# Linear attention in 64-token blocks instead of 128, inside a fused attention and MLP kernel

## The chip, the cores and the metric

The kernel runs on one core of a Trainium2 chip. The metric is the device time of one execution in microseconds; lower is better. The kernel before took 193.41 us (median of three runs, 192.16 to 193.62).

The names of the engines in the profile: PE is the matrix engine (PEld its weight loads), DVE the vector engine, ACT the scalar (activation) engine, POOL the GpSimd engine, SP the engine that issues most transfers. PSUM is the memory that PE writes into, in banks; SBUF is the working memory.

## What is computed

Four batches, eight heads, 768 tokens, head size 64. A decaying linear attention, written in blocks of 64 tokens, feeds an MLP of width 512 to 2048 to 512 with a quick GELU:

```python
block = 64
rel = pos[:, None] - pos[None, :]
Dmask = np.where(rel >= 0, lam[:, None, None] ** rel[None, :, :], 0.0)
lam_pow = lam[:, None, None] ** (pos[None, :, None] + 1)
for b in range(nb):
    intra = np.einsum('bhic,bhjc->bhij', qb, kb) * Dmask[None]
    intra = np.einsum('bhij,bhjd->bhid', intra, vb)
    inter = np.einsum('bhid,bhde->bhie', qb * lam_pow[None], kv_state)
    out[:, :, sl] = intra + inter
    rev_pow = lam[:, None, None] ** (block - 1 - pos[None, :, None])
    kv_state = lam_block * kv_state + np.einsum('bhsd,bhse->bhde', kb * rev_pow, vb)
x = attention output, (3072, 512)
h = x @ w_in                              # 512 to 2048
out = (h * sigmoid(1.702 * h)) @ w_out    # 2048 to 512
```

The block length is a free choice: a longer block moves work from the state into the masked scores, with the same result.

## The kernel before

The 3072 tokens are worked in six waves of 512. Waves 0 and 1 take 256 tokens of two batches each and have functions of their own (names with d_). Waves 2 to 5 take 128 tokens of all four batches; their functions begin with n_ and are what the change touches. Matrices are in bf16, sums in f32 in PSUM.

**Attention of a wave (2 to 5).** Heads are laid out in pairs on the 128 partitions, rows A = 0 to 63 and Z = 64 to 127. One block is the whole 128 tokens.
- `n_scores` (L335): for each of four head pairs p, eight matmuls that contract over 64 rows and give scores of 128 x 128 tokens for one batch and one head.
- `n_masks` (L345): scores times a power of lambda for each row (inv_pow) and a triangle of ones and zeros. There are two ways: "M" does it in one DVE instruction (L354), "m" scales on ACT (L350) and multiplies on DVE (L351).
- `n_rest` (L377): state times q (inter, L383), masked scores times v on top of it in the same PSUM bank (intra, `n_out`, L396), ACT copies the result to xT (L400), and then `n_state` (L363) sums keys times values over all 128 tokens (L370) and DVE adds this to the decayed old state (L374). The state is held twice (kv_sb) and written for the next wave.

**MLP of a wave.** Both products are done as seven products of halves with sums before and after (a Strassen form). The first: four groups a, b, c, d, each with products 1 to 7 (`in_product`, L548; matmuls at L561) and a GELU (A to D, `in_gelu`, L580). The second: `product` (L454, matmuls at L470) with n = 1 to 7 and t = 0, 1 for two token halves. Its sums of g are made on DVE ("gl1" to "gl4" for the low, "gh1" to "gh4" for the high half, L447). Its banks are Q (product 2), V (7, then 4 on top) and X (1, 6, 5, 3, one on top of the other). So product 5 may only add into X when product 6's value has been copied out of it, and product 3 when product 5's has been read. `after_product` (L480) does the copies on ACT (products 1, 6, 7, L486) and the sums on DVE (2, 4, 5, L502); a sum of product 4 waits there for the copy of product 6, and product 2's sum is put off to the step "o". Outputs leave through SP (L510).

**What sets the order.** The order on every engine is written out by hand: `STEPS[w]` (L633) lists for wave w the products of its MLP between the attention steps of wave w + 1. Each engine runs its instructions in that order and waits where data or a buffer are not ready. The letters: "a1", "b7" and so on are products of the first matmul, "P40" is product 4 for t = 0, "S" and "M" or "m" are scores and masks, "v0", "v1" the casts of v to bf16 for batches 0, 1 and 2, 3 (both on ACT, L224), "R" is `n_rest`, "K", "Q", "t" prepare the next k and q, "L" issues loads, "X" makes sums of xT for the next MLP ("+a1" is that next wave's product).

PSUM is handed out in two rings: tag "a" with five banks (scores, attention outputs, states, some products) and "mm" with three.

Of the kernel before, what the change touches and what calls it, by code (L numbers as in the profile page):

```python
# [25 lines left out]
def kernel(  # L26
# [13 lines left out]
    nc = tc.nc  # L40
# [3 lines left out]
    P = 128  # L44
# [67 lines left out]
    def iota(x, pattern, base, cm):  # L112
        nc.gpsimd.iota(x, pattern=pattern, base=base, channel_multiplier=cm, allow_small_or_imprecise_dtypes=True)
# [20 lines left out]
    iota(i_q, [[0, 1]], 1, 1)  # L134
    mask = work.tile([P, 1, P], bf16, tag="mask", bufs=1, name="mask")
    nc.gpsimd.memset(mask, 1.0)
# [30 lines left out]
    inv_pow = const.tile([P, H], f32)  # L167
    blk_pow = const.tile([P, NP], f32)
    warm = const.tile([P, 1], f32)
# [124 lines left out]
    def d_keep(w, c):  # L294
        nc.scalar.copy(kv_sb[1][:, 2 * w + c], states[w, c])
        if w:
            kept[w, c] = work.tile([P, NP, D], f32, tag="half", bufs=1, name="half")
            nc.scalar.copy(kept[w, c], states[w, c])
# [36 lines left out]
    def n_scores(w, p):  # L335
        s2 = [acc("ps_s") for _ in range(2)]
        for b in range(B):
            kT, qT = trans[w, b // 2, "k"], trans[w, b // 2, "q"]
            for h in range(2):
                hs = slice(64 * h, 64 * h + 64)  # L340
                nc.tensor.matmul(s2[h][:, b, :], kT[hs, (b % 2) * NP + p, :], qT[hs, (b % 2) * NP + p, :],  # L341
                                 start=True, stop=True)
        masked[w, p] = s2

    def n_masks(w, p, split=False):  # L345
        for h, s in enumerate(masked.pop((w, p))):
            sm = work.tile([P, B, P], bf16, tag="sm", bufs=8, name="sm")
            n = 4 * (p // 2) + 2 * h + p % 2
            if split:
                nc.scalar.activation(sm, s, COPY, scale=inv_pow[:, n : n + 1])  # L350
                nc.vector.tensor_tensor(sm, sm, mask.to_broadcast([P, B, P]), op=MUL)  # L351
                masked[w, p, h] = sm
                continue
            nc.vector.scalar_tensor_tensor(sm, s, inv_pow[:, n : n + 1],  # L354
                                           mask.to_broadcast([P, B, P]), op0=MUL, op1=MUL)
            masked[w, p, h] = sm

    def n_two(w, pp):
        for f in (n_scores, n_masks):
            for p in (2 * pp, 2 * pp + 1):  # L360
                f(w, p)

    def n_state(w, R):  # L363
        ps_kv = acc("ps_kv", shape=[P, 2, B, D])
        new, old = kv_sb[(w + 1) % 2], kv_sb[w % 2]
        for i in range(2):
            for b in range(B):
                for j, js in enumerate((A, Z)):
                    n0 = (2 * R + i) * P + j * D
                    nc.tensor.matmul(ps_kv[js, i, b, :], cast[w, b // 2, "k"][:, b % 2, n0 : n0 + D],  # L370
                                     v_sb[w % 2][:, b, 4 * R + 2 * j + i, :], start=True, stop=True)
        for i in range(2):
            p = 2 * R + i
            nc.vector.scalar_tensor_tensor(new[:, :, p, :], old[:, :, p, :], blk_pow[:, p : p + 1], ps_kv[:, i],  # L374
                                           op0=MUL, op1=ADD)

    def n_rest(w):  # L377
        kv, o = kv_sb[w % 2], [acc("ps_o") for _ in range(NP)]
        for R in range(2):
            for b in range(B):  # L380
                for i, cs in enumerate((A, Z)):
                    for j, js in enumerate((A, Z)):
                        nc.tensor.matmul(o[2 * R + j][cs, b, :], kv[js, b, 2 * R + i, :],  # L383
                                         trans[w, b // 2, "q"][js, (b % 2) * NP + 2 * R + i, :],
                                         start=(b == 0), stop=False, skip_group_check=True)
        for p in range(NP):
            n_out(w, p, o[p])
        if w + 1 < NW:
            for R in range(2):
                n_state(w, R)  # L390

    def n_out(w, p, ps_o):
        vt, R, j = v_sb[w % 2], p // 2, p % 2
        for b in range(B):
            for i, cs in enumerate((A, Z)):
                nc.tensor.matmul(ps_o[cs, b, :], vt[:, b, 2 * p + i, :], masked[w, 2 * R + i, j][:, b, :],  # L396
                                 start=False, stop=True, skip_group_check=True)
        if w not in xT:
            xT[w] = xp.tile([P, NP, W], bf16, tag="x", name="xT")
        nc.scalar.copy(xT[w][:, p, :], ps_o.rearrange("p b s -> p (b s)"))  # L400
# [181 lines left out]
    def one_step(w, s):  # L582
# [30 lines left out]
        elif s[0] == "m":  # L613
            n_masks(x, int(a), True)
        elif s[0] == "R":
            n_rest(x)
# [13 lines left out]
        else:  # L630
# [27 lines left out]
    with tc.manual_schedule():  # L658
        for x, i in ((k_pow, i_k), (q_pow, i_q)):
            nc.scalar.activation(x, ln_lam.unsqueeze(1).to_broadcast([P, 2, H]), EXP, scale=i)  # L660
        mk_pow(inv_pow, -1.0 * P)
# [39 lines left out]
        for pp in range(2):  # L701
            d_scores(0, 1, pp)
            d_masks(0, 1, pp)
        nc.gpsimd.affine_select(mask, mask, pattern=[[0, 1], [1, P]], channel_multiplier=-1, base=0,
                                compare_op=mybir.AluOpType.is_ge, fill=0.0)
# [116 lines left out]
```

## Time and profile before

| what | value |
| --- | --- |
| median of three runs | 193.41 us |
| profiled execution | 193.18 us |
| its span | 191.4 us |
| one wave, from one first score stretch to the next (94.07 to 122.10) | 28.03 us |
| busy in that wave: PE, DVE, ACT, POOL | 28.03, 24.62, 20.81, 8.23 us |

How to read the lines below. The page's first part gives each engine's busy time, its share of the span and the number of instructions; the second shows busy tenths in 40 equal slices. The chain of waits goes back from the last instruction to whatever released it: start, length, engine, tile and line, count. A row of the timeline has start, length, engine, line, operation, output and inputs, count, and in brackets the engine's idle time before it and who ended it. A row of a group has its count, then busy time in all and the mean length of one in ns, then idle time before. PE matmuls overlap, so the mean length of one is longer than the step from one to the next.

### The profile page before, as it was taken

Reading aid. Unit: us, or ns where it says so; the run is one execution under the profiler, and the core shown is the slowest. Engines: PE = TensorE matmul, PEld = TensorE weight load, DVE = VectorE, ACT = ScalarE, POOL = GpSimd, SP = SyncE. Lnnn points to the kernel's source line nnn. Section 1 sums busy time; section 2 is a strip of 40 time slices with the busy share of each in tenths; the row PEclk is TensorE's granted clock in tenths of the full one; section 3 lists DMA queues with packets and bytes.
Section 4 is the critical chain, followed back from the end, with each engine's and each line's share of the span. In section 5 each row is a group of like instructions: output and inputs, shape, how many; then the busy total and the mean of one; then the engine's idle time right before and its main releaser. Section 6 shows DMA issues by size and latency. Waiting matters only on the chain.

```text
span 191.4 us, 5525 instructions
## 1 busy us (share of the span) xinstructions
PE 184.1 (96%) x2295; PEld 151.9 (79%) x2295; DVE 152.0 (79%) x282; ACT 129.9 (68%) x242; POOL 51.2 (27%) x69
## 2 busy tenths in 40 slices
PE   7888999999999999999999999999999999999993
PEld 2556646877888888888888888888888888888882
DVE  3687289997965799879799879799789797888950
ACT  6766764168776986389896288885488876597611
POOL 5588000046449000195000294000493000000000
PEclk9999999999999999999999999999999999999999
DMA  5999999996998899768999455999365803300113
GB/s 144 320 281 194 203 206 204 284 312 178 232 265 184 193 225 255 191 161 154 218 233 229 165 146 132 224 254 254 107 156 126 202 4 113 110 5 0 54 58 110
DMA packets 89599, 33.91 MB, mean 177 GB/s; under 512 B 67430, under 2 KB 89446, under 8 KB 89574
## 3 DMA queue, kind: packets, MB, share of 16 engines
q1 hardware_dynamic: 84676, 28.84, 60.4%
q0 software_dynamic: 4896, 4.72, 14.5%
q8 instruction: 18, 0.29, 0.6%
q14 instruction: 7, 0.06, 0.1%
q10 hardware_dynamic: 2, 0.00, 0.0%
HBM read 27.26 MB, written 6.29 MB: 175 GB/s over the span
## 4 chain that ended last, share of the span: by engine, by line
PE 76%; DMA 9%; DVE 8%; POOL 3%; ACT 1%; SPq 1%; issue 0%; ACTq 0%
PE ps_X L470 20%; PE ps_hX L561 16%; PE ps_V L470 9%; PE ps_hV L561 8%; DMA w_in<-in_moe_w_in_dram 7%; PE ps_Q L470 5%; PE ps_hQ L561 4%; PE ps_h L420 4%; DVE w_out_t L434 3%; DVE g_s L447 3%; DMA qf<-in_q_dram 2%; PE ps_s L341 2%; PE ps_o L396 2%; POOL w_in L184 2%; PE ps_o L383 1%; DVE w_in_t L537 1%
## 5 line engine op out<-in xcount | busy, mean ns | idle before, releaser
L470 PEld LDWEIGHTS <-g_s 128*128 128x128 bf16 x384 | 37.0, 98 | 4.8
L580 ACT ACTIVATE g_sb<-h_sb 128x512 bf16<-128x512 f32 x54 | 32.6, 631 | 1.2 <-DVE h_sb L569 1.2
L470 PEld LDWEIGHTS <-g_sb 128*128 128x128 bf16 x288 | 27.5, 98 | 4.4 <-issue 0.3
L561 PEld LDWEIGHTS <-w_in_t 128*128 128x128 bf16 x288 | 28.1, 98 | 3.3
L224 ACT COPY part<-ps_hX 128x512 f32<-128x512 f32 x32 | 18.3, 586 | 11.5 <-PE ps_hX L561 11.5
L470 PE MATMUL ps_X<-w_out_t,g_s 128*128 128x256 bf16 x192 | 23.3, 273 | 0.0
L561 PEld LDWEIGHTS <-w_in 128*128 128x128 bf16 x216 | 21.1, 98 | 2.5
L561 PE MATMUL ps_hX<-x_s,w_in_t 128*128 128x256 bf16 x144 | 21.6, 272 | 0.0
L447 DVE TENSOR_TENSOR g_s<-g_sb 128x1024 bf16<-128x1024 bf16 x24 | 16.2, 686 | 5.8 <-ACT g_sb L580 5.6
L212 POOL TENSOR_TENSOR ks<-kf,k_pow 128x512 bf16<-128x512 f32 x16 | 16.3, 1042 | 4.5 <-DMA kf<-in_k_dram 4.5
L212 POOL TENSOR_TENSOR qs<-qf,q_pow 128x512 bf16<-128x512 f32 x16 | 16.7, 1069 | 2.7 <-DMA qf<-in_q_dram 2.7
L221 DVE COPY part<-ps_hV 128x512 f32<-128x512 f32 x18 | 12.4, 688 | 5.9 <-PE ps_hV L561 5.9
L653 POOL CAST behind_q<-x_s 1x1 f32<-1x1 bf16 x3 | 0.5, 176 | 58.5 <-DVE x_s L546 58.5
L486 ACT COPY part<-ps_X 128x512 f32<-128x512 f32 (+1 forms) x13 | 6.7, 518 | 13.5 <-PE ps_X L470 13.5
L569 DVE TENSOR_TENSOR h_sb<-part,ps_hX 128x512 f32<-128x512 f32 x18 | 12.2, 680 | 2.6 <-PE ps_hX L561 2.1
L569 DVE TENSOR_TENSOR h_sb<-part,ps_hV 128x512 f32<-128x512 f32 x18 | 12.3, 683 | 1.0 <-PE ps_hV L561 1.0
L470 PE MATMUL ps_X<-w_out,g_sb 128*128 128x256 bf16 x96 | 12.6, 272 | 0.2 <-DMA w_out<-in_moe_w_out_dram 0.2
L470 PE MATMUL ps_Q<-w_out,g_sb 128*128 128x256 bf16 x96 | 12.5, 273 | 0.0
L569 DVE TENSOR_TENSOR h_sb<-part,ps_hQ 128x512 f32<-128x512 f32 x18 | 12.2, 678 | 0.0
L224 ACT CAST v_sb<-vf 128x1024 bf16<-128x1024 f32 (+1 forms) x14 | 11.9, 866 | 0.2 <-DMA vf<-in_v_dram 0.2
L580 ACT ACTIVATE g_sb<-ps_hX 128x512 bf16<-128x512 f32 x18 | 10.6, 588 | 1.8 <-PE ps_hX L561 1.8
L420 PE MATMUL ps_h<-xT,w_in 128*128 128x256 bf16 x96 | 11.3, 273 | 0.3 <-DMA w_in<-in_moe_w_in_dram 0.3
(113 smaller groups left out, 354.1 us busy)
## 6 DMA issues: line engine op xcount, KB each, us to landing
kf<-in_k_dram SPq DMA_DIRECT2D x10, 512.0 KB, 6.6
qf<-in_q_dram SPq DMA_DIRECT2D x10, 512.0 KB, 6.7
vf<-in_v_dram SPq DMA_DIRECT2D x10, 512.0 KB, 6.1
out_dram<-o_sb SPq DMA_DIRECT2D x24, 128.0 KB, 2.5
out_dram<-o_sb SPq DMA_DIRECT2D x12, 256.0 KB, 2.5
w_out<-in_moe_w_out_dram POOLq DMA_DIRECT2D x4, 512.0 KB, 15.4
kf<-in_k_dram SPq DMA_DIRECT2D x4, 256.0 KB, 3.1
qf<-in_q_dram SPq DMA_DIRECT2D x4, 256.0 KB, 4.5
```

Of the source, the lines that this page charges most:

```text
L184: nc.gpsimd.dma_start(out=w_in_sb[j], in_=moe_w_in.rearrange("(kc ki) f -> ki kc f", ki=P)[:, :, c0 : c0 + IN_CH[j] * P])
L212: eng.tensor_tensor(x.rearrange("p b (r i j d) -> p j (b r) i d", i=2, j=2, d=D)[:, j], f.rearrange("p h (a d) -> p (h a) d", a=2).rearran ...
L221: nc.vector.tensor_copy(out, in_)
L224: nc.scalar.copy(out, in_)
L420: nc.tensor.matmul(h[:, u, :], w_in_sb[j][:, kc, i * P : (i + 1) * P], xT[w][:, kc, cols], start=(kc == 0), stop=(kc == KC - 1))
L434: nc.vector.tensor_tensor(o, x, y, op=SUB)
L447: nc.vector.tensor_tensor(o, x, y, op=f)
L470: nc.tensor.matmul(bank[:, t], x[:, m, t * P : (t + 1) * P], y, start=((n in (1, 2, 7) or own) and t == ts[0] * last and m == 0), stop=(m ...
L486: nc.scalar.copy(part[w, n, t.start][:, t], bank[:, t])
L561: nc.tensor.matmul(bank[:, u], z[:, kc], y[:, kc], start=(n in (1, 2, 7) and u + kc == 0), stop=(kc == 1), skip_group_check=True)
L569: nc.vector.tensor_tensor(h, h_part[w, g, {2: 1, 5: 7, 4: 6}[n]], bank, op=ADD)
L580: nc.scalar.activation(g_of[w][:, a : b + 1 : b - a, 256 * i : 256 * i + 256], bank, GELU)
```

## The change

Attention of waves 2 to 5 goes to blocks of 64 tokens. Scores are 64 x 64 for each of the two blocks (a wave has both blocks of all pairs in two calls, one stretch, "S0 S1"), with all masks in one DVE multiply for each tile by a ready table (`mask`, now f32 for every head; POOL makes it near the start from inv_pow). State sums get a stretch of their own, "T", with sums for each block apart. "F" makes a middle state (old state decayed plus the first block's sum; two DVE instructions and one ACT copy to bf16), "N" adds the second block's sum to give the next wave's state (DVE). "R" has four units of 32 matmuls: inter for both blocks (the second from the middle state), then intra. Between them ACT reads one column of two banks (`seen`), so that the last unit adds into a bank only after the first unit's sums are in. The results go to xT by ACT for the first block and DVE for the second. In the last wave's attention only the first block's sum is made, where there was no state before.

In STEPS, gl1 and gl2 go ahead of gh3, the second score stretch is gone, v0 and v1 follow P21, T follows P40, R stands between P60 and P61, and o, gl4 and gh4 stand behind P61. The last line of STEPS (5) is the same but for its line breaks.

```diff
-    def n_scores(w, p):
-        s2 = [acc("ps_s") for _ in range(2)]
-        for b in range(B):
-                nc.tensor.matmul(s2[h][:, b, :], kT[hs, (b % 2) * NP + p, :], qT[hs, (b % 2) * NP + p, :],
...
+    def n_scores(w, pp):
+        s2 = [acc("ps_s", shape=[P, 2, B, D]) for _ in range(2)]
+        for i in range(2):
+            for b in range(B):
+                kT, qT = trans[w, b // 2, "k"], trans[w, b // 2, "q"]
+                r = (b % 2) * NP + 2 * pp + i
+                for bs in (A, Z):
+                    for h, hs in enumerate((A, Z)):
+                        nc.tensor.matmul(s2[h][bs, i, b, :], kT[hs, r, bs], qT[hs, r, bs], start=True, stop=True)
+        masked[w, pp] = s2
...
+            nc.vector.tensor_tensor(sm, s, mask[:, n : n + 2].unsqueeze(2).to_broadcast([P, 2, B, D]), op=MUL)
...
+    def n_state(w):
+        ts = (A, Z) if w + 1 < NW else (A,)
+        for R in range(2):
+            for t in range(len(ts)):
+                kv_ps[w, t, R] = acc("ps_kv", shape=[P, 2, B, D])
+            for i in range(2):
+                for b in range(B):
+                    for j, js in enumerate((A, Z)):
+                        n0 = (2 * R + i) * P + j * D
+                        for t, rows in enumerate(ts):
+                            nc.tensor.matmul(kv_ps[w, t, R][js, i, b, :], cast[w, b // 2, "k"][rows, b % 2, n0 : n0 + D],
+                                             v_sb[w % 2][rows, b, 4 * R + 2 * j + i, :], start=True, stop=True)
+
+    def n_mid(w, R):
+        half = kv_half[w, R] = op.tile([P, 2, B, D], f32, tag="o", name="kv_half")
+        mid = kv_mid[w, R] = work.tile([P, 2, B, D], bf16, tag="sm", bufs=8, name="kv_mid")
+        for i in range(2):
+            p = 2 * R + i
+            nc.vector.scalar_tensor_tensor(half[:, i], kv_sb[w % 2][:, :, p, :], blk_pow[:, p : p + 1],
+                                           kv_ps[w, 0, R][:, i], op0=MUL, op1=ADD)
+        nc.scalar.copy(mid, half)
+
+    def n_new(w, R):
+        new = kv_sb[(w + 1) % 2][:, :, 2 * R : 2 * R + 2, :].rearrange("p b i d -> p i b d")
+        nc.vector.tensor_tensor(new, kv_half[w, R], kv_ps[w, 1, R], op=ADD)
+
+    def n_rest(w, copies):
+        o = [[acc("ps_o", shape=[P, 2, B, D]) for _ in range(2)] for _ in range(2)]
+        def unit(*parts):
+            for R in range(2):
+                for b in range(B):
+                    for i, cs in enumerate((A, Z)):
+                        for rows, (kind, blk, j) in zip((A, Z), parts):
+                            r = 2 * R + i
+                            if kind == "inter":
+                                x = kv_mid[w, R][rows, i, b, :] if blk else kv_sb[w % 2][rows, b, r, :]
+                                y = trans[w, b // 2, "q"][rows, (b % 2) * NP + r, (A, Z)[blk]]
+                            else:
+                                x, y = v_sb[w % 2][rows, b, 4 * R + 2 * j + i, :], masked[w, R, j][rows, i, b, :]
+                            nc.tensor.matmul(o[blk][j][cs, R, b, :], x, y,
...
+        unit(("inter", 1, 0), ("inter", 0, 1))
+        for t in (o[1][0], o[0][1]):
+            nc.scalar.copy(seen, t[:, 1, B - 1, D - 1 : D])
+        unit(("inter", 0, 0), ("inter", 1, 1))
+        unit(("intra", 0, 0), ("intra", 1, 1))
...
+        for i in range(2):
+            to_x(i, i)
+        unit(("intra", 0, 1), ("intra", 1, 0))
+        for i in range(2):
+            to_x(i, 1 - i)
...
     STEPS = {
...
-        3: ("a7v a6 G K0 tk0 b1 b7v A2 a5 b2 b6 a4 A5 a3 c1 A4 K1 tk1 B2 b5 c7v c2 c6 B5 b3 b4 d1v Q0 tq0 c5 "
-            "B4 C2 d7v d2 d6 D2 c3 c4 Q1 tq1 Lw Lk d5 d4 P10 C4 d3 C5 D4 P11 gl3 D5 gh3 S0 S1 M0 P20 m1 gl1 "
-            "P70 P71 gl2 P21 v0 gh12 S2 S3 M2 m3 v1 o P40 P41 P60 gl4 gh4 P61 R P50 P51 +a1 X +a2 P30 P31 "),
+        3: ("a7v a6 G K0 tk0 b1 b7v A2 a5 b2 b6 a4 A5 a3 c1 A4 K1 tk1 B2 b5 c7v c2 c6 B5 b3 b4 d1v Q0 tq0 c5 B4 "
+            "C2 d7v d2 d6 D2 c3 c4 Q1 tq1 Lw Lk d5 d4 P10 C4 d3 C5 D4 P11 gl3 gl1 gl2 D5 gh3 S0 S1 M0 P20 M1 P70 "
+            "P71 P21 v0 v1 gh12 P40 T F0 F1 P41 P60 N0 N1 R P61 o gl4 gh4 P50 P51 +a1 X +a2 P30 P31"),
...
-        nc.gpsimd.affine_select(mask, mask, pattern=[[0, 1], [1, P]], channel_multiplier=-1, base=0,
-                                compare_op=mybir.AluOpType.is_ge, fill=0.0)
+        nc.gpsimd.tensor_copy(mask, inv_pow.unsqueeze(2).to_broadcast([P, H, D]))
+        for r in (A, Z):
+            nc.gpsimd.affine_select(mask[r], mask[r], pattern=[[0, H], [1, D]], channel_multiplier=-1, base=0,
+                                    compare_op=mybir.AluOpType.is_ge, fill=0.0)
```

More of the change, by code (lines that the diff above doesn't have):

```diff
@@ L133 @@
     i_q = const.tile([P, 1], f32)
-    iota(i_q, [[0, 1]], 1, 1)
-    mask = work.tile([P, 1, P], bf16, tag="mask", bufs=1, name="mask")
-    nc.gpsimd.memset(mask, 1.0)
+    iota(i_q[A], [[0, 1]], 1, 1)
+    iota(i_q[Z], [[0, 1]], D + 1 - P, 1)
+    mask = work.tile([P, H, D], f32, tag="mask", bufs=1, name="mask")
     fill_ps = {}
@@ L166 @@
     q_pow = const.tile([P, 2, H], f32)
-    inv_pow = const.tile([P, H], f32)
+    early = op.tile([P, 2, 256], f32, tag="part", bufs=6, name="early")
+    inv_pow, warm = early[:, 0, 0:H], early[:, 1, 0:1]
     blk_pow = const.tile([P, NP], f32)
-    warm = const.tile([P, 1], f32)
     behind_q = const.tile([1, 1], f32)
@@ L296, in d_keep @@
         if w:
-            kept[w, c] = work.tile([P, NP, D], f32, tag="half", bufs=1, name="half")
+            kept[w, c] = work.tile([P, NP, D], f32, tag="sm", bufs=8, name="half")
             nc.scalar.copy(kept[w, c], states[w, c])
@@ L333, in d_x @@
         copy(xT[w][:, :, n0 : n0 + P], t)
-    def n_scores(w, p):
-        s2 = [acc("ps_s") for _ in range(2)]
-        for b in range(B):
[L338 to L356, printed above, removed]
@@ L392, in n_out @@
[L392 to L397, printed above, removed]
+            nc.vector.scalar_tensor_tensor(half[:, i], kv_sb[w % 2][:, :, p, :], blk_pow[:, p : p + 1],
+                                           kv_ps[w, 0, R][:, i], op0=MUL, op1=ADD)
@@ new lines, in n_mid, with to_x @@
+        nc.scalar.copy(mid, half)
[5 more added lines that the diff above has]
+        def unit(*parts):
+            for R in range(2):
+                for b in range(B):
[8 more added lines that the diff above has]
+                            nc.tensor.matmul(o[blk][j][cs, R, b, :], x, y,
+                                             start=(kind == "inter" and R + b == 0), stop=(kind == "intra"),
+                                             skip_group_check=True)
+        def to_x(blk, j):
+            copies[blk](xT[w].rearrange("p (r j) (b k s) -> p j k r b s", j=2, k=2, b=B)[:, j, blk], o[blk][j])
+        unit(("inter", 1, 0), ("inter", 0, 1))
[3 more added lines that the diff above has]
+        unit(("intra", 0, 0), ("intra", 1, 1))
@@ L660 @@
             nc.scalar.activation(x, ln_lam.unsqueeze(1).to_broadcast([P, 2, H]), EXP, scale=i)
-        mk_pow(inv_pow, -1.0 * P)
+        for rows, e in ((A, -1.0 * P), (Z, 0.0)):
+            nc.scalar.activation(inv_pow[rows], ln_lam[rows], EXP, scale=e)
         for j, rows in enumerate((A, Z)):
```

44 lines of the change are left out of this document (14 added, 30 removed), and 24 rows, old and new, of the table STEPS.

## The prediction

> **What bounds the kernel now.** I read the page first (busy shares, the 40 slices), then the chain of waits over one whole wave, then the timeline of ACT and DVE around that wave's attention.
>
> ```profile
> span 191.4 us, 5525 instructions
> PE 184.1 (96%) x2295; PEld 151.9 (79%) x2295; DVE 152.0 (79%) x282; ACT 129.9 (68%) x242; POOL 51.2 (27%) x69
> ...
> PE   7888999999999999999999999999999999999993
> ```
>
> PE is busy in nearly every one of the 40 slices. The profiled run took 193.18 us, of which 191.4 is span; the median of the three runs is 193.41, 0.23 above it. My sum is made against 193.18. The chain of waits for one wave (MLP of wave 2, attention of wave 3) is nothing but PE:
>
> ```profile
> 94.07 0.55 PE ps_s L341 x16
> 94.62 0.98 PE ps_Q L470 x8
> 95.60 1.75 PE ps_V L470 x16
> 97.35 0.87 PE ps_Q L470 x8
> 98.22 0.55 PE ps_s L341 x16
> 98.77 1.85 PE ps_V L470 x16
> 100.63 1.75 PE ps_X L470 x16
> 102.37 0.57 PE ps_o L383 x32
> 102.94 1.01 PE ps_o L396 x32
> 103.96 0.50 PE ps_kv L370 x32
> 104.46 1.85 PE ps_X L470 x16
> ...
> 107.19 1.81 PE ps_X L470 x16
> ...
> 122.10 0.55 PE ps_s L341 x16
> ```
>
> From 94.07 to 122.10 no other engine ends a wait, so PE time saved in attention is gained in full, and any new wait of PE is lost in full. Attention is 0.55 + 0.55 + 0.57 + 1.01 + 0.50 = 3.18 us of each wave. The rows between are products: 16 matmuls of 256 columns take 1.75 (0.109 each); right behind small matmuls a product costs 0.10 more (0.98 for 0.87, 1.85 for 1.75).
>
> **The small matmuls.** Today: 64x128 pairs in the scores, 64x64 in the inter part (L383), 128x64 pairs in the intra part (L396), all 128 columns wide, and 128x64 pairs of 64 columns in the state (L370). After: everything is 64x64 tiles with 64 columns, four tiles of the array to a group. A wave has 64 + 64 + 128 = 256 such matmuls, 64 groups: 16 in S0 S1, 16 in T, 32 in R. No row shows four tiles with 64 columns, so I bound a group. L396 (16 groups of two) less L383 (8 groups of four) is 0.44 us for 8 groups: 55 ns for a group of 128 columns, the rest of each row, about 0.12, being the start of a stretch. S (8 pairs in 0.55) says the same, so 55 ns holds whether two tiles or four run. L370 has 16 groups of 64 columns in 0.50: 31.5 ns, and no start, as the tile shape before it is the same. Columns set the price, the number of tiles does not: I take 31.5 ns. The upper end is 55 ns, as if 64 columns cost what 128 do; the lower end is the streaming rate, 64 columns at 109/256 ns, 27 ns.
> After, at 31.5: S 0.12 + 0.51 = 0.63, T 0.63, R 0.12 + 1.01 = 1.13, sum 2.39. Saving 0.79 a wave. In the last attention (wave 5) there was no state before, so 2.68 stands against 2.39 (its T is 16 pairs at the price of L370): saving 0.29. The extra 0.10 of a product behind small matmuls occurs three times before (P20, P40, P50) and three times after (P20, P41, P61).
>
> The Trainium skill (TensorE: Matmul & The Clock Gate, section Back-to-back issue gap) speaks against the change: it lists a floor of about 25 ns from one matmul to the next for 1 to 64 columns; by it 256 matmuls would be 6.4 us a wave and the time about 215. The trace disagrees with it already for two tiles, 15.6 ns a matmul in L370.
>
> **The waits that the new order makes.** I lay the new order on the clock of this wave, with these rows:
>
> ```profile
> 97.38 0.59 ACT L486 COPY part<-ps_V 128x512 f32<-128x512 f32 x1 [0.36 <-PE ps_V L470]
> 97.87 1.05 ACT L224 CAST v_sb<-vf 128x1024 bf16<-128x1024 f32 x1
> 98.81 1.27 ACT L350 ACTIVATE sm<-ps_s,inv_pow 128x512 bf16<-128x512 f32 x2
> 99.96 1.05 ACT L224 CAST v_sb<-vf 128x1024 bf16<-128x1024 f32 x1
> 102.41 0.59 ACT L486 COPY part<-ps_X 128x512 f32<-128x512 f32 x1 [1.39 <-PE ps_X L470]
> ```
> ```profile
> 94.90 0.69 DVE L447 TENSOR_TENSOR g_s<-g_sb 128x1024 bf16<-128x1024 bf16 x1 [1.37 <-ACT g_sb L580]
> ...
> 102.73 1.28 DVE L447 TENSOR_TENSOR g_s<-g_sb,g_s 128x1024 bf16<-128x1024 bf16 x2
> 103.94 0.68 DVE L502 TENSOR_TENSOR o_sb<-part,ps_V 128x512 f32<-128x512 f32 x1
> 104.54 1.65 DVE L374 SCALAR_TENSOR_TENSOR kv<-kv,blk_pow,ps_kv 128x256 bf16<-128x256 bf16 x4
> 106.35 0.69 DVE L502 TENSOR_TENSOR o_sb<-part,ps_X 128x512 f32<-128x512 f32 x1 [0.17 <-PE ps_X L470]
> ```
> ```profile
> L470 PE MATMUL ps_X<-w_out_t,g_s 128*128 128x256 bf16 x32 | 3.8, 273 | 0.0
> ...
> L569 DVE TENSOR_TENSOR h_sb<-part,ps_hX 128x512 f32<-128x512 f32 x4 | 2.7, 680 | 0.6 <-PE ps_hX L561 0.6
> ...
> L370 PE MATMUL ps_kv<-v_sb,ks 128*64 128x64 bf16 x32 | 0.7, 196 | 0.0
> ```
>
> Spacing on an engine is less than an instruction's duration: the v cast gives ACT back after 98.81 - 97.87 = 0.94, a copy after 97.87 - 97.38 = 0.49, the g sums go every 1.28 - 0.68 = 0.60 on DVE, the four state updates every (1.65 - 0.47)/3 = 0.39.
>
> *1. v.* P71 ends at 97.35 + 0.08 = 97.43. Behind it on ACT stand the copy of V (97.46), then both casts: v0 at 97.95, v1 at 98.89 to 99.94. T needs v_sb; today the state comes at 103.96, long after. Now it comes right behind P21 and P40, at 97.43 + 1.74 = 99.17. Its third group is the first for batches 2 and 3 and needs v1; it would end at 99.17 + 0.12 + 3 x 0.0315 = 99.39, but PE is let go at 99.99 and a matmul of L370 takes 0.20: 100.19. Wait: 0.80. The trace has a wait of this kind once, a state product in an early wave behind its v cast, and it shows 0.05 from the cast's end (46.19 + 1.14) to PE:
>
> ```profile
> 46.19 1.14 ACT L224 CAST v_sb<-vf 128x512 bf16<-128x512 f32 x2
> ...
> 47.38 0.41 PE L285 MATMUL ps_kv<-v_sb,ks 64*64 64x64 bf16 x14 [0.28 <-ACT v_sb L224]
> ```
>
> *2. The middle state.* T's first half ends at 100.19 + 5 x 0.0315 = 100.35, all of it at 100.60. DVE is free by then: the masks, now four multiplies out of PSUM like the additions of L569 (0.68, one every 0.60), follow gh3 (94.90, so from 95.5) and end near 98.0, gh12 near 99.2; gl1 and gl2, moved up, fit in the 1.37 idle before gh3. F0 and F1 are four updates from 100.39; the last is done at 100.39 + 3 x 0.39 + 0.47 = 102.03. ACT's second copy, at the 0.59 of the copies above, lets PE go at 102.71. PE has P41 and P60 (0.97 + 0.87) until 102.44, starts R, and its fifth group would end at 102.73; with its weight load (0.1, as bounded by the 109 ns step of the products) and matmul (0.2) it ends near 103.03. Wait: 0.3. N0 (DVE, 101.95 to 102.63) frees the PSUM bank of R's second unit just in time; the two one-column copies on ACT, at most a spacing of 0.49 each, hide behind units two and three (0.5) or cost a few tenths at the most. R ends at 103.03 + 27 x 0.0315 = 103.9.
>
> *3. Bank X.* Today R's 2.1 us stand between P61 and P50, and hide the copy of X by ACT (102.41 to 103.00): P50 adds into the bank that the copy reads. Now R comes before P61, and P50 follows P61 at once. P61 ends at 103.9 + 0.97 = 104.87, the copy takes 104.91 to 105.50, P50 starts at 105.55. Its first matmul would have started 0.109 behind P61's last, at 104.87 - 0.27 + 0.11 = 104.71. Wait: 0.84.
>
> *4. DVE before P30.* P30 adds into X too, after the sum of product 5 has read it. Today that sum starts 0.04 behind P51's end and P30 waits 0.06 (1.81 for 1.75). In the new queue of DVE it stands behind four others, all but the first moved here: the sum of product 4 (which needs the copy of step 3), product 2's, gl4, gh4. They start at 105.54; the sum of product 5 at 105.54 + 4 x 0.60 = 107.94, done 108.62, and PE goes at 108.67. PE has P50 P51 until 107.46 and two products of a (107.19 less the end of P51, 104.46 + 1.85: 0.88): P30 would start at 108.18. Wait: 0.49.
>
> After P30 the order is as before. The two copies of R to xT on DVE (0.60 each) stand ahead of that queue and end near 105.2.
>
> **Costed at nothing.** The wider mask: POOL makes it early, and is busy 27% of the span. One more EXP on ACT at the start, before PE's stream begins. ACT loses four scalings and two copies a wave and gains two copies: slack there, but not where the v casts stand. DVE gains two additions and two copies a wave and loses four multiplies; even without the loss that is 4 x 0.60 = 2.4, and it is busy 24.6 of 28.0 us:
>
> ```profile
> 94.07:122.10 28.03, 28.03 (x354) 24.50 (x356) 24.62 (x44) 20.81 (x38) 8.23 (x9) 1.00 0.77 188
> ```
>
> (DVE is the third busy figure.) No load, cast by POOL or transpose is moved. Product 2's and 4's output transfers are issued some 3 us later on SP; its next load stands in the next wave's second half, and nobody waits for these.
>
> **The sum.** A wave: waits 0.80 + 0.30 + 0.84 + 0.49 = 2.43, less the 0.06 that P30 waits already, less 0.79: +1.58. Three waves +4.74; the last attention 2.37 - 0.29 = +2.08. Total +6.82: 193.18 + 6.82 = 200.0 us.
>
> **Rivals.**
> B, PE itself becomes dearer: a group of four tiles costs 55 ns at 64 columns. Then S and T take 1.00, R 1.88, sum 3.88: 0.70 more than today. Wait 2 shrinks to some 0.1, the others stay: 2.19. Three waves of 0.70 + 2.13, the last 3.51 - 2.68 + 2.13 (its T is pairs): +11.4, 204.6 us. For it: no row has four tiles at 64 columns. Against: the price has followed the columns everywhere. Chance 0.21.
> C, an issue floor for each matmul: if L370's 15.6 ns is a floor and not its columns, a group of four costs 62.5 ns; S and T 1.12, R 2.12, sum 4.36, the last wave 3.87. Three times 1.18 + 2.13 and 1.19 + 2.13: +13.2, 206.4 us. Against: L383 ran 32 matmuls in 0.57, at 13.8 each without its start. Chance 0.05; the skill's 25 ns above is the same rule, harsher.
> D, some waits are covered: only waits 1 and 3 stay, and at 0.65 each, because casts and copies go faster than their rows. 3 x (1.30 - 0.79) + 1.30 - 0.29 = +2.5, 195.7 us. Chance 0.07. With waits of 0.7 a wave it comes out even (within 1%): 0.03.
> E, faster: ACT frees v and X before PE arrives, so PE keeps its stream and only the saving counts: 3 x 0.79 + 0.29 = 2.7 less, 190.5 us. It decides where a wave's waits stay below some 0.6. Against: in the changed kernel's instruction order P50's first matmul waits for the copy directly before it, whatever ACT's load. Chance 0.04.
>
> **How the numbers follow.** My forecast, the four waits with groups near 31.5 ns, has 0.60 and gives 200.0. The range leaves out E, the even case, D and C (0.04 + 0.03 + 0.07 + 0.05) and takes in B's 204.6 and, below, the 27 ns group (1.1 less) together with waits a fifth smaller (1.8 less): 197.3 to 205.0. A measurement of this kernel tells about 1% from no change. Faster by over 1%: 0.04; within 1%: 0.04; slower: 0.92.
>
> **What would show it.** Right: in the chain of waits of the new profile, each wave has ACT v_sb ahead of the state matmuls, ACT part<-ps_X between two ps_X stretches, and DVE o_sb ahead of the last ps_X; the distance from one score stretch to the next grows from 28.03 to about 29.6; 64 score matmuls take about 0.6. If they take 1.0, B is right. Wrong: score stretches 28.0 or less apart, or no idle PE between P61 and P50. If the largest wait stands elsewhere (masks late on DVE, say), my reading of the queues failed.

## The result, and the profile after

The changed kernel takes 204.38 us (median of four runs, 203.95 to 204.53) against 192.86 for the kernel before on the same chip: ratio 1.0593, 95% interval 1.0540 to 1.0646. The forecast was 200.0 us, with a range of 197.3 to 205.0: the direction and the kind of loss were foreseen, and the time was 4.4 us too low. Below, the profiled execution of after (203.95 us, span 202.16) stands against that of before (193.18, span 191.40): 10.8 us of span.

From the page of after: the totals, PE's row in the 40 slices, its granted clock, and the queue that brings the instructions.

```profile
span 202.2 us, 6554 instructions
PE 185.6 (92%) x2805; PEld 151.7 (75%) x2807; DVE 156.6 (77%) x284; ACT 123.6 (61%) x235; POOL 52.3 (26%) x71
...
PE   7689999999999968999988999988999978999993
...
PEclk9999999999999988999999999999999999999999
...
q8 instruction: 22, 0.36, 0.8%
```

PE falls from 96% of its span to 92%, with a dent in each of the four attention stages (the 6, the 88s and the 7), and one dent in the clock as well. The chain of waits of after, for the wave whose chain before stands in the prediction (MLP of wave 2, attention of wave 3):

```profile
98.52 0.67 PE ps_s L343 x64
99.18 0.98 PE ps_Q L483 x8
100.16 1.76 PE ps_V L483 x16
...
102.43 2.00 ACT v_sb L224 x2
104.43 0.04 issue
104.47 0.66 PE ps_kv L365 x56
105.14 0.98 PE ps_V L483 x8
106.11 0.87 PE ps_X L483 x8
106.99 0.25 PE ps_o L395 x16
...
107.27 1.21 PE ps_o L395 x112
108.48 0.99 PE ps_X L483 x8
...
109.49 0.59 ACT part L499
...
110.11 1.29 DVE o_sb L515 x2
```

What was nothing but PE now has the casts of v ahead of the state sums (L365), the copy of bank X behind P61, and the DVE sum ahead of P30. The list of waits of after, PE alone (total us, times, longest us):

```profile
PE ps_kv L365 <- ACT v_sb L224: 4.4, 4, 2.0
PE ps_X L483 <- ACT part L499: 2.7, 4, 0.7
...
PE ps_X L483 <- DVE o_sb L515: 1.4, 4, 0.3
```

The list counts idle time from the end of the last matmul. What the stream loses is more, since matmuls overlap: from the start of one to the start of the next, less the usual step, the copy of X costs 0.84 each time and the DVE sum 0.51. With losses measured that way, and the score stretches starting at 65.89, 98.45, 128.20 and 158.14 (before: 65.96, 94.00, 122.04, 150.07), each wave comes out like this (us against before):

| | wave 2 | wave 3 | wave 4 | wave 5 | predicted |
|---|---|---|---|---|---|
| wait 1, v | 2.18 | 0.79 | 0.79 | 1.32 | 0.80 |
| half clock behind it | 1.54 | 0 | 0 | 0 | none |
| wait 2, middle state | 0 | 0.19 | 0.19 | 0.20 | 0.30 |
| wait 3, bank X | 0.84 | 0.84 | 0.84 | 0.84 | 0.84 |
| wait 4, DVE, less the 0.06 before | 0.45 | 0.45 | 0.45 | 0.45 | 0.43 |
| scores wait for a transpose of q | 0 | 0 | 0.17 | 0 | none |
| PE's own work (the remainder) | -0.49 | -0.56 | -0.53 | -0.11 | -0.79 (-0.29) |
| to the next scores, or to the end | +4.52 | +1.71 | +1.91 | +2.70 | +1.58 (+2.08) |

The four sums make 10.84; wave 2 starts 0.07 earlier, so 10.8. This is one execution. Of the four, two have a mean granted clock of 0.992 (203.95 and 204.53 us, the first of them profiled) and two of 1.0 (204.44 and 204.33). One stretch of 3.4 us at half clock is worth 0.008 of that mean, so the half clock isn't in every run, and the runs without it are no faster. No trace shows what they lose in its place.

**Where wave 2 went.** The chain of waits there begins at a transfer:

```profile
64.51 7.69 DMA vf<-in_v_dram
...
72.22 1.05 ACT v_sb L224
...
73.32 0.66 PE ps_kv L365 x56
73.98 1.82 PE ps_V L483 x8
```

The second half of v lands at 72.20. ACT is ready for it 1.25 us earlier and PE stands for 2.02. Then comes a second loss: the product behind the state sums, 8 matmuls of 256 columns, takes 1.82 where it takes 0.98 in wave 3's chain. The same stretch in the view by windows (us, then PE, PEld, DVE, ACT and POOL busy, granted clock, DMA share, GB/s):

```profile
70.44:73.85 3.41, 1.39 (x71) 1.06 (x68) 0.83 (x3) 1.58 (x2) 0.00 (x0) 1.00 1.20 222
73.85:77.27 3.42, 3.42 (x30) 2.26 (x17) 2.75 (x6) 1.24 (x2) 0.00 (x0) 0.50 1.20 221
```

From 73.85 to 77.27 the granted clock is 0.50: fifteen matmuls go at 0.213 us instead of 0.109. In wave 5 the load is late again, at a smaller price (chain of after):

```profile
155.03 8.53 DMA vf<-in_v_dram
...
163.59 1.05 ACT v_sb L224
```

Before's trace has the second load of v of wave 2 landing at 69.99, 6.2 us after its issue, and that of wave 5 at 154.73 (issued at 147.0; the view by tiles gives 7.8 to landing). Measured from their score stretches they land 4.0 and 4.7 us in; after, 6.3 (72.20 - 65.89) and 5.4 (163.56 - 158.14). Wait 1 had put the second cast 4.9 us in (98.89, with the score stretch starting at 94.00). The loads met that with 0.9 and 0.2 to spare, and nothing in the prediction looked at it.

### The profile page after: what moved, and what is told of

Read it like the earlier page. It is cut to its first block, busy times and chain, and to the rows that moved or that the text cites. A ratio compares the mean times of both kernels' runs of the same rounds, so it can differ in the third digit from the quotient of the medians.

```text
span 202.2 us, 6554 instructions
## 1 busy us (share of the span) xinstructions
PE 185.6 (92%) x2805; PEld 151.7 (75%) x2807; DVE 156.6 (77%) x284; ACT 123.6 (61%) x235; POOL 52.3 (26%) x71
## 3 DMA queue, kind: packets, MB, share of 16 engines
q1 hardware_dynamic: 84676, 28.84, 64.4%
## 4 chain that ended last, share of the span: by engine, by line
PE 37%; DMA 20%; issue 13%; POOL 11%; SPq 7%; DVE 5%; ACT 3%; POOLq 1%; ACTq 0%
PE ps_X L483 9%; DMA vf<-in_v_dram 8%; PE ps_hX L574 6%; DMA qf<-in_q_dram 6%; POOL qs L212 6%; PE ps_h L421 5%; PE ps_V L483 4%; SPq L84 4%; POOL ks L212 4%; DMA kf<-in_k_dram 4%; PE ps_hV L574 3%; DVE o_sb L515 3%; PE ps_o L395 2%; ACT v_sb L224 2%; DMA out_dram<-o_sb 2%
## 5 line engine op out<-in xcount | busy, mean ns | idle before, releaser
L483 PE MATMUL ps_X<-w_out_t,g_s 128*128 128x256 bf16 x192 | 24.8, 279 | 2.7 <-ACT part L499 2.7
L483 PE MATMUL ps_X<-w_out,g_s 128*128 128x256 bf16 x96 | 11.6, 272 | 1.4 <-DVE o_sb L515 1.4
L221 DVE CAST xT<-ps_o 128x512 bf16<-128x512 f32 x10 | 6.5, 688 | 7.5 <-PE ps_o L395 4.6
```

What stands on the lines that cost most here:

```text
L221: nc.vector.tensor_copy(out, in_)
L483: nc.tensor.matmul(bank[:, t], x[:, m, t * P : (t + 1) * P], y, start=((n in (1, 2, 7) or own) and t == ts[0] * last and m == 0), stop=(m ...
```

## The experiments

The theory after the result: the loss is the four waits of the prediction, and on top of them a load that lands too late and the slow clock behind a long wait. Rivals: that PE's smaller tiles cost more than they seem and the waits only show it; that the wait for v is a matter of the load's place in SP's queue and can be had for nothing by issuing it earlier; that a stream of such small matmuls has a limit of its own which the waits hide. Each run has the kernel before beside it on its chip; the step strings are those of waves 2 to 5, cut to the steps that change. In the ratios, brackets hold the 95% interval. From here on a wait for v, or a stop inside R, is given as the whole time from one start to the next, 0.03 more than in the table; the others are given less the usual step, as there.

**1. r_last: R behind P61.** It removes waits 3 and 4 by moving PE's cover, and leaves wait 1.

```diff
- P40 T F0 F1 P41 P60 N0 N1 R P61 o gl4 gh4 P50 P51
+ P40 T F0 F1 P41 P60 N0 N1 gl4 gh4 P61 R o P50 P51
```

> The changed kernel with one edit: R stands behind P61 again (P41 P60 N0 N1 gl4 gh4 P61 R o P50), v stays late. My theory (PE loses the copy of bank X, 0.84 a wave, and the queue of DVE before P30, 0.4 to 0.5 a wave, and in three waves 0.2 for the middle state): 5 to 6 us less than the changed kernel's 204.4, so 198.5 to 199.5. Rival, the 64-column tiles and their switches are what costs: nothing of that moves, 203.5 to 204.5.

Measured: 199.05 us, ratio 1.0346 [1.0263, 1.0429], 5.3 us below after, or 4.8 when each is set against the kernel before on its own chip (192.33 here). Waits 3 and 4 are gone from the list (4 x 1.29 = 5.2 in the table); smaller terms moved with them. The wait for v stays, 2.53 in wave 2 and 0.83 in the others, with 1.21 us of slow clock behind the long one. Wave 5's load was in time here. Two rows of the list of waits are new: scores of wave 2 that wait 0.64 for a late transpose of q, and the second row here:

```profile
PE ps_kv L365 <- ACT v_sb L224: 4.2, 4, 2.3
...
PE ps_X L483 <- issue: 0.7, 1, 0.7
```

"Issue" means that PE waited for nothing the profile knows. That row becomes the question of runs 5 to 11.

**2 to 4. v_load, v_early, both: the load of v first.** v_load issues v's loads at the start of a wave's steps instead of behind the transposes of k and q (wave 2's, which the stage before issues, ahead of its last products). v_early also casts v ahead of P70, and both is v_early with the order of r_last. (The last pair of lines is v_early and both only; in wave 1 these two also issue Lk, the loads of k and q, behind the casts.)

```diff
- 3: ("a7v a6 G K0 tk0
+ 3: ("Lw a7v a6 G K0 tk0
...
- Q1 tq1 Lw Lk d5 d4
+ Q1 tq1 Lk d5 d4
...
- M1 P70 P71 P21 v0 v1 gh12 P40
+ M1 v0 v1 P70 P71 P21 gh12 P40
```

> The changed kernel with v's loads issued at the start of each wave's steps (for wave 2 ahead of the last eight half products), casts where they are. Theory: in wave 2 the load landed late (the trace shows ACT waiting 1.25 us for it) and PE stood 2.02 us, behind which sixteen product matmuls took twice their time (1.6 us more); in wave 5 PE stood 1.16. With v there in time each wave keeps only the wait for the casts, 0.6 to 0.8: 1.2 + 1.6 + 0.5 = 3.3 less, 201.1. Rival, the halved clock comes from the 64x64 stretches and not from the wait: only 1.7 less, 202.7. Rival, the load is not what is late: 204.4.

> As v_load, and both v casts stand ahead of the copy of V on ACT (M1 v0 v1 P70 P71). Theory: no wait for v is left in any wave, 4.4 of idle PE, about 0.8 of pipeline refill and 1.6 of slow clock: 6 to 7 less, 197.5 to 198.5. Rival, the queue of ACT only moves the wait: the copy of V is late by the casts and P40 waits for it instead, some 0.5 a wave: 199.5 to 200.5.

> r_last and v_early together: 64-token blocks with none of the new waits. Theory: the saving of PE alone is left, 0.79 in three waves and 0.29 in the last, so 2.7 less than before: 190.0 to 190.7, a ratio near 0.986, and score stretches about 27.25 apart. Rival, the small tiles cost more than their rows say (switches, weight loads): 192.5 to 194.5, no gain over before.

Measured: 213.72 us (1.1108 [1.1062, 1.1154]), 211.63 (1.0975 [1.0910, 1.1041]) and 205.81 (1.0686 [1.0644, 1.0728]). All three missed: the wait for v shrinks to 0.83 a wave (v_load) or goes (the other two), and a greater one takes its place. From v_load's list of waits (both has 8.8 in the first row too):

```profile
PE ps_s L343 <- DMA qT<-qs: 8.8, 6, 2.4
...
PE ps_kv L365 <- ACT v_sb L224: 2.6, 4, 0.7
```

SP's queue shows why. After's timeline of SP (start, us, instruction), then v_load's:

```profile
58.29 1.42 SPq L248 DMA_TRANSPOSE kT<-ks  x1
59.81 1.27 SPq L248 DMA_TRANSPOSE qT<-qs  x1
...
62.54 1.29 SPq L248 DMA_TRANSPOSE qT<-qs  x1
63.88 2.57 SPq L88 DMA_DIRECT2D vf<-in_v_dram  x2
```
```profile
58.12 2.38 SPq L88 DMA_DIRECT2D vf<-in_v_dram  x2
60.61 3.30 SPq L248 DMA_TRANSPOSE kT<-ks  x1
...
66.73 1.28 SPq L248 DMA_TRANSPOSE qT<-qs  x1
```

The load of v takes 2.4 us of SP and the transpose behind it holds SP for 3.30 instead of 1.42, so the last transpose of q is issued 4.2 us later, when the scores should be running. It is no single case: in the three traces all twelve transposes right behind a load of v hold SP for 3.2 to 4.3 us, and none elsewhere for more than 2.4. The place of the load was not free: the transposes are due first. The rival that it could be had for nothing falls for this place; a place between the transposes was not tried.

**5. dve_first: only DVE's queue.** The two weight-sum steps gl4 and gh4 go ahead of R, R stays ahead of P61. This should take wait 4 and leave wait 3.

```diff
- P41 P60 N0 N1 R P61 o gl4 gh4 P50 P51
+ P41 P60 N0 N1 gl4 gh4 R P61 o P50 P51
```

> The changed kernel with gl4 and gh4 ahead of R, and o behind P61's sum (P41 P60 N0 N1 gl4 gh4 R P61 o P50); R still stands before P61. Theory: only the wait of DVE's queue before P30 goes (0.51 in each of four waves in the trace), the one for the copy of X stays: 2.0 less than the changed kernel's 204.4, 202.4. Rival, the lateness only moves from the sum of product 5 to the copies to xT, and the next wave's first product waits: 204.4.

Measured: 202.54 us, 1.0556 [1.0498, 1.0615]. Wait 4 is gone in all four waves (0.51 to 0), and wait 3 stays at 0.84, so these two are separate, as the prediction had them. Behind a wait for v of 2.67 the clock stayed at full speed this time, and inside R of wave 2 PE stopped for 1.06 us without a releaser. From its list:

```profile
PE ps_X L483 <- ACT part L499: 2.7, 4, 0.7
...
PE ps_o L395 <- issue: 0.9, 1, 0.9
```

**6. t_late: r_last, with T behind P41.** One product more of PE's own work ahead of T.

```diff
- P40 T F0 F1 P41 P60 N0 N1 R P61 o gl4 gh4 P50 P51
+ P40 P41 T F0 F1 P60 N0 N1 gl4 gh4 P61 R o P50 P51
```

> As r_last, and T stands behind P41 instead of P40, 0.87 us later: P40 P41 T F0 F1 P60 N0 N1 gl4 gh4 P61 R o P50. Loads are untouched. Theory: the v casts are done when T comes in waves 3 and 4 (0.8 each gone), wave 2 keeps about 1.6 of 2.5 us, wave 5 nothing to 0.4, the middle state stays hidden behind two products or costs 0.3: 199.0 less 3 to 3.5, 195.6, and 194.2 if a shorter wait in wave 2 leaves the clock alone. Rival, the state sums cost their price wherever they stand: 199.

Measured: 197.89 us, 1.0320 [1.0277, 1.0364]. The wait for v is gone in waves 3 to 5, and stays in wave 2 at 2.06. Not all of it came back: the interval overlaps r_last's. An "issue" stop of 0.77 and a wait for R's copies of 0.65 (a1 <- DVE xT) are new, and 0.94 us of slow clock remains.

**7. t_late_gate: t_late, with wave 1's loads of k and q (for wave 3) held back until the first half of v has been cast**, to learn whether they slow v's.

```diff
- M1 Lk P70 P71 P21 v0 v1
+ M1 P70 P71 P21 v0 Y Lk v1     (Y: a small transfer on SP that reads v_sb)
```

> As t_late, and in wave 1's steps the loads of k and q for wave 3 are held back on SP until wave 2's first v cast is done (a tiny transfer that waits for it). Theory: those loads share the transfer engines with wave 2's v and make it land late; alone, v lands some 2 us sooner, PE's wait in wave 2 falls below 0.5 and the clock is not lowered: 2 to 3 us less than t_late, 192 to 193, level with before or just under it. Rival, v is late for another reason: as t_late. Rival, the held loads come too late for wave 3: worse than t_late, with scores of wave 3 waiting.

Measured: 199.03 us, 1.0370 [1.0290, 1.0449]. The wait in wave 2 falls from 2.06 to 1.16 and no slow clock follows, as the theory had it; but the time is no better than t_late's. Two stops without a releaser, 1.97 inside R of wave 2 and 1.71 behind R of wave 3, took the gain:

```profile
PE ps_o L395 <- issue: 1.8, 1, 1.8
PE ps_X L483 <- issue: 1.5, 1, 1.5
```

Nor is it shown that the held loads had slowed v's. Its second half takes 7.61 us from issue to landing here, against 8.39 in t_late, but 7.69 in after and 8.01 in r_last, where those loads are in place. Why it takes 6.22 in the kernel before, with the loads of k behind it just the same, stays open.

**8. hold: r_last, with 3, 6 and 12 one-column copies on ACT between the two casts of v of waves 3, 4 and 5** (they write a scratch column that nothing uses), to see from which wait the clock drops.

```diff
- v0 v1
+ v0 Y3 v1      (wave 3; Y6 in wave 4, Y12 in wave 5)
```

> As r_last, with 3, 6 and 12 one-column copies on ACT between the v casts of waves 3, 4 and 5, which make PE's wait in T longer by about 0.19 for each (0.6, 1.1, 2.3 over 0.8; these copies compute nothing). Asks when a wait of PE is followed by products at half speed, as behind the 2 us wait of wave 2. Theory (the wait itself lowers the clock, from some 2 us on): full speed behind 1.4, half speed behind 3.1, and 1.9 tells the edge. Rival (something else in wave 2, such as the transfers): full speed behind all three.

Measured: 206.70 us (one run). The waits for v are 2.61, 1.36, 2.03 and 3.37 us. The windows behind the last three:

```profile
104.00:108.00 4.00, 4.00 (x155) 3.46 (x152) 4.00 (x9) 2.27 (x6) 0.00 (x0) 1.00 1.30 223
...
133.50:137.50 4.00, 4.00 (x77) 3.11 (x70) 3.71 (x8) 1.24 (x2) 0.00 (x0) 0.66 1.15 218
...
166.00:170.00 4.00, 4.00 (x44) 3.02 (x44) 2.86 (x6) 1.24 (x2) 0.00 (x0) 0.50 0.01 4
```

Full speed behind 1.36, 0.66 behind 2.03, 0.50 behind 3.37; and full speed again behind wave 2's 2.61. Among the waits for v of all runs the half clock followed those of 2.03, 2.06, 2.21, 2.53 and 3.37, not those of 2.61 and 2.67, and none under 1.7. So the length alone does not decide. The traces show what does: within each of them all changes of the granted clock lie whole steps of 3.413 us apart, wherever the waits fall, and what counts is how much idle time of PE falls into one step. Two steps of this run, the one with most of wave 2's wait and the one with wave 4's (PE's busy time is the first figure behind the length):

```profile
69.95:73.36 3.41, 1.70 (x22) 1.25 (x21) 1.02 (x2) 1.77 (x3) 0.00 (x0) 1.00 1.11 190
...
131.39:134.80 3.41, 1.57 (x72) 1.35 (x69) 1.01 (x3) 1.89 (x7) 0.00 (x0) 1.00 1.19 222
```

PE is idle for 1.71 us of the first step, and the next one is at full clock; it is idle for 1.84 of the second, and the next one is at half. With the steps laid over all 13 traces, each step at full clock that held 1.84 or more was followed by one at half clock, and none that held 1.71 or less was. The idle time in run 5's 2.67 was cut by a step's edge into 1.47 and 1.00. The Trainium skill (TensorE: Matmul & The Clock Gate, section What's actually happening) says that the clock is halved after about one idle window of 3.4 us, and that the window runs freely. The free run and the length agree with these steps; a window that is idle throughout is not needed, 1.84 us of 3.41 were enough.

**9. t_after_p6: T and R both behind P61**, with the sum of product 4 put off (e), so that all four waits have cover.

```diff
- P40 T F0 F1 P41 P60 N0 N1 R P61 o gl4 gh4 P50 P51 +a1 X +a2 P30 P31
+ P40 P41 P60 gl4 gh4 P61 T F0 F1 N0 N1 P50 P51 e R P30 P31 +a1 X o +a2
```

> 64-token blocks in an order made for them: P40 P41 P60 gl4 gh4 P61 T F0 F1 N0 N1 P50 P51 e R P30 P31 +a1 X o +a2, where e is the sum of product 4, put off behind P51. T stands between P61 and P50 (hides the copy of X but for 0.2), P50 P51 hide the middle state, R hides the sum of product 5, P30 P31 hide the copies to xT; v has 3.5 us more than in the changed kernel. Theory: per wave some 0.3 to 0.5 of waits against 0.79 saved, no half clock: 191.0 to 192.0 where before is near 192.3, a ratio of 0.993 to 1.0. Rival, PE runs out of instructions (the idle put down to issue in the profiles of t_late and t_late_gate, 0.7 to 1.9 us at a place): 193 to 195.

Measured: 196.34 us, 1.0206 [1.0161, 1.0251], above both ranges that were expected. None of the four waits is left beyond some hundredths, and it is still slower than before. Its list of waits, the rows of the attention waves:

```profile
PE ps_o L395 <- issue: 1.3, 2, 1.0
...
PE ps_hQ L574 <- issue: 0.5, 1, 0.5
...
PE ps_s L343 <- DMA qT<-qs: 0.5, 1, 0.5
```

The score stretches are 28.84, 28.78 and 28.64 apart, for 28.04 before. Stops without a releaser cost 0.56 and 1.15 in the R of waves 2 and 3 and 0.70 behind wave 4's, and late transposes of q 0.64 and 0.28. Without them the three waves would be 27.6 to 27.7: PE's own saving is 0.4 a wave, half of the 0.79 predicted (the table's 0.49 to 0.56 leaves out a seam of 0.12 in R, which it counts as wait 2), and in the last wave nothing.

**10. t_six_times: t_late, with the state sums of waves 3 and 4 done six times over** (each pass overwrites the same sums): 384 small matmuls and 384 weight loads in a row, to see the stop by itself.

```diff
-             for i in range(2):
+             for i in [0, 1] * (6 if w in (3, 4) else 1):
```

> As t_late, with the state matmuls of waves 3 and 4 made six times over, 384 in one stretch (the repeats overwrite the same sums). Theory A, a group of four costs 31.7 ns and nothing else: 96 groups, 3.1 us a stretch. Theory B, PE outruns the fetch of its instructions (256 at a time; the trace shows about 2.6 us from the start of a fetch to the first instruction after the idle): the first 300 or so instructions run at 31.7 ns a group, then PE waits for each further 256, and the 768 take 5 to 8 us with idle put down to issue. Theory C, the array needs more for each group in the long run: an even pace above 31.7.

Measured: 218.13 us (one run). At the price of a group the stretch is 3.1 us. It took 10.2 in wave 3, the later part of it at half clock, and in wave 4 its pieces look like this (timeline of PE; the last number is idle time):

```profile
142.36 1.68 PE L365 MATMUL ps_kv<-v_sb,ks 64*64 64x64 bf16 x181
147.12 1.26 PE L365 MATMUL ps_kv<-v_sb,ks 64*64 64x64 bf16 x128 [3.08 <-issue]
151.40 1.23 PE L365 MATMUL ps_kv<-v_sb,ks 64*64 64x64 bf16 x75 [3.01 <-issue]
```

After the first 181, PE runs 128 matmuls, that is 256 instructions with their weight loads, in 1.1 us, stops, and resumes 4.3 us after it last resumed (3.5 in wave 3). On the page, the instruction queue carries 27 packets in 0.44 MB here:

```profile
q8 instruction: 27, 0.44, 0.9%
```

Before's page has 18 and 0.29, after's 22 and 0.36: 16 KB each, one more for each 256 instructions that PE gained (2295 + 2295 before, 2805 + 2807 after). In the trace each such packet takes 0.9 to 1.5 us and PE resumes some 2.6 us after it started (dve_first: 75.66 to 78.34). The same holds for every stop in the traces of all runs that is put down to issue, lies in waves 2 to 5 and is over 0.1 us: there are 16, between products as well as within R and T, and each ends 2.3 to 2.9 us after a packet's start. The stops are PE out of instructions. The Trainium skill (Runtime: NRT & Kernel Launch, section Instruction fetch mechanics) has the blocks of 16 KiB or 256 instructions, and the trace agrees; it also calls their fetch hidden behind the pace of issue, and these rows do not agree.

**11. r_split: t_after_p6, with R cut in two around P30**, no matmul more or less.

```diff
- P50 P51 e R P30 P31 +a1 X o +a2
+ P50 P51 e R P30 R P31 +a1 X o +a2     (inter units, then intra units)
```

> The order of t_after_p6 with R cut in two stretches of 64 matmuls: its inter units stay behind P51 and the sum of product 4, its intra units go behind P30 (... P50 P51 e R P30 R P31 ...). No matmul is added or removed. In t_after_p6 PE stopped three times with no engine named as the releaser, 0.56 us inside R of wave 2, 1.15 inside R of wave 3 and 0.70 just behind wave 4's, each in or behind the 256 instructions of R (128 matmuls and 128 weight loads in 1.42 us). Theory, instruction blocks of 256 come too slowly for a stretch that uses one up in 1.4 us, and a stop ends some 2.6 us after a fetch began: now a block lasts about 0.75 + 0.98 + 0.5 = 2.2 us at its densest, so no stop may be longer than about 0.4, all stops with that releaser together at most 0.8 instead of 2.4. New seams cost about 0.2 a wave (0.1 for each start of a stretch and each product behind one), and the first product of the next wave's first half may wait some 0.3 for the last copy of R: 0.8 + up to 0.9 more. Span 192.7 to 194.2 beside 193.4. Rival, the stops are tied to something else at these places (a bank, a semaphore, the switch from inter to intra units): they stay 0.5 to 1.2 each, and the span is 194.2 to 195.5.

Measured: 198.47 us, 1.0319 [1.0282, 1.0356]. No stop without a releaser is left among PE's waits, as the theory has it, but the time missed its range: P30 now comes before DVE has read bank X, the next wave's first products come before R's last copy, and a later product of it waits for a sum on DVE (h_sb).

```profile
PE ps_X L484 <- DVE o_sb L516: 1.6, 3, 0.5
...
PE ps_hX L575 <- DVE h_sb L583: 1.1, 4, 0.3
PE ps_hX L575 <- DVE xT L221: 0.7, 4, 0.2
```

Since the wait for DVE stands in the very stretch where a stop stood, it also gives the fetch its time: the run fits the theory and does not prove it alone. Run 10 and the 16 stops carry it.

## Why the prediction was right, and where it failed

- **The price of a group held.** 31.5 ns for four 64x64 tiles with 64 columns was right: the starts of a stretch step by 31.7 ns per group, and 64 score matmuls take 0.67 us in the chain, where the forecast said 0.63 and rival B 1.00. Rivals B and C fall. The 25 ns per matmul that the prediction cited from the Trainium skill (TensorE: Matmul & The Clock Gate, section Back-to-back issue gap) do not hold for these tiles: a group of four steps by 31.7, some 8 ns a matmul.
- **The saving was mis-sized.** 0.79 a wave was forecast, 0.49 to 0.56 came; the last wave gave 0.11 for 0.29. S takes 0.67 and T 0.67 (run 6) for 0.63 each, and R, less its wait, about 1.27 for 1.13 (0.25 + 1.21 in the chain, less 0.19): a change from inter to intra units and of the bank inside R costs some hundredths each time, which the term "0.12 for the start" of one stretch left out. That is about 1.0 us of the miss. The 0.2 at R's fifth group isn't all a wait for the middle state either: with the state long done, in waves 3 and 4 of run 9, a seam of 0.12 stays there.
- **Waits 3 and 4 were right** in place and size: 0.84 for 0.84, 0.45 for 0.43. Wait 2 is 0.19 for 0.30, and up to 0.12 of that is the seam. Runs 1 and 5 take 3 and 4 away, together and one alone, and the time follows.
- **Wait 1 is the step that failed.** In waves 3 and 4 it is 0.79 for 0.80, as laid out on wave 3's clock. That clock was then used for all four waves. The sentence "No load, cast by POOL or transpose is moved" was true of the order of issue and took the load's landing as given, though the new order used up its lead. In the kernel before, ACT came to the second half 1.9 us (wave 2) and 1.3 us (wave 5) after it had landed, and PE took v up only 3 us after that (L396, 102.94 on wave 3's clock); the new order left 0.9 and 0.2. The load of wave 2 then landed 2.2 us later on the trace's clock: 0.7 because SP came to it later, 1.5 because the transfer took 7.69 for 6.2, the cause of which stays open (run 7). Price: 1.38 in wave 2 and 0.52 in wave 5 beyond the forecast.
- **A cost that no step had**: the half clock behind the 2.02 us of idle PE, 1.54 us in the profiled execution.
- Summed: 1.38 + 0.52 + 1.54 + 0.17 (scores) + 1.0 (saving) less 0.6 (wait 2, and wave 2 has none) is 4.0, the 10.8 measured less the 6.82 forecast.
- **The range held partly by luck.** Its upper part was there for rival B, dearer groups of matmuls, and B did not happen. The 204.38 us lie in that part mostly because of a late load and the slow clock behind it (1.38 + 0.52 + 1.54 of the 4.0 us), which no term of the range stood for.
- **Rival D**, waits partly covered, did not happen in after, and runs 1, 6 and 9 show what it would bring: 199.05, 197.89 and 196.34 as more of them are covered. **Rival E**, faster, was wrong beyond its odds: it priced a kernel without waits at 190.5. Run 9 has none of the four and takes 196.34: PE runs out of instructions (2.4 us), the transposes of q come late (0.9), and the saving is 0.4 a wave. No order tried beats the kernel before, and PE's saving of 0.4 a wave leaves little to win.

## What to carry to other kernels

When an operation is moved ahead, write down for every wave, not for one, when each of its inputs lands in the old trace, and how much of that lead the move uses up: a load with less than 1 us to spare is a wait to come, and a load moved ahead on a shared queue takes its time from what it passes. Splitting matmuls into smaller tiles saves array time but doubles the instructions, so price a stretch of them twice, by its columns and by how fast its instructions can arrive; and look at each removed wait for what it had been hiding. An idle PE of about 1.8 us or more may cost half the clock for the next 3.4 us or longer as well, depending on where it falls.

## What the runs showed of the hardware

- A long stretch of small matmuls is fed 256 instructions at a time: 128 matmuls with their loads run in 1.1 us, and PE resumed 4.3 us (once 3.5) after it had last resumed (run 10). Each of 16 stops ended 2.3 to 2.9 us after the start of a 16 KB instruction packet. Stops of 0.6 to 2.0 us of the same kind appeared in the kernel itself as soon as PE had no other wait around R (runs 1, 5, 6, 7 and 9).
- The granted clock changed only at steps of 3.413 us, fixed for one execution. Behind a step at full clock with 1.84 us or more of idle PE came one at half clock, behind one with 1.71 or less none did, in all 13 traces. Behind five of the seven waits for v of 2.03 us and more this cost 0.9 to 2.4 us each.
- A transpose issued right behind a load of v on SP held the queue 3.2 to 4.3 us in twelve of twelve cases (runs 2 to 4); elsewhere transposes took 1.2 to 2.4.
